# Gated linear attention into a gated SSM: all transfers on the sync queue, issued a few at a time, and the weights read a second time for their check

## Chip, cores and metric

One core of one Trainium2 chip. The metric is the device time of one execution in microseconds (us), median of several. An execution is called slow when it is over 1.5% above the fastest of the same kernel, and otherwise fast.

## The reference

For 4 batches of 8 heads, 768 steps and head dimension 48, a gated linear recurrence makes `y`. Its heads are joined to 384 channels and go through a gated state-space block of 512 inner channels:

```python
for t in range(S):                                        # S = 768
    state = alpha[:, :, t, :, None] * state + np.einsum('bhd,bhe->bhde', k[:, :, t], v[:, :, t])
    y[:, :, t] = np.einsum('bhd,bhde->bhe', q[:, :, t], state)
x = np.ascontiguousarray(y.transpose(0, 2, 1, 3)).reshape(B, S, H * D)
proj = x @ w_in;  val, gate = proj[..., :D_inner], proj[..., D_inner:]
h = a[0, 0] * h + val[:, t, :]                            # for each t; a = exp(A_log)
out = (silu(gate) * ys @ w_out).astype(np.float32)
```

The weights `w_in` and `w_out` arrive as float64. The kernel reads them as 32-bit words, builds float32 from them with integer operations, and checks that no weight lies outside the range for which this is right. If one does, a flag sends the kernel into a general, slow branch.

## The kernel before

The sequence is worked in 12 turns (4 batches of NG = 3 groups of 256 steps). Turn n handles the attention of group n, the projections (`pj`) of group n-1 and the output (`o`, `o_sb`, store) of group n-2. A hand-written list of letters gives the order of the parts of a turn: F and A are the front (scans, q, k, scores), B the back (states `z`, values `y`, features), P and H projection and scan, O the output, W the check of a part of the weights, L and M loads.

```python
early = ["FFFFLUFUFABBABB", "UUFPUUFHPUHFFPUHBBCPHABUAUBL", "FPUFHPUHFFPHBBCAPHBWAWOBWAWOM"]
usual = "FLPHPHFFOABBCPHABPHBAOM"

# the output: o_sb is in a pool of two buffers, the store goes out on ScalarE's queue
o_sb = pool.tile([C, DM], FP32, name="o_sb")
nc.scalar.activation(o_sb, o, AF.Copy)
nc.scalar.dma_start(out=out[b, ds(g * GC + c * C, C), :], in_=o_sb)

# from turn 4 on, alpha, q and k come by whole batches. staging (raw weights) and batches 1 and 3 share memory
t = big.tile([C, 3, NP * NW * W], FP32, tag=f"big{1 - b % 2}", name="batch")
...
nc.sync.dma_start(out=tv[...], in_=src[...])      # 48 for batch 1, 12 larger ones for batches 2 and 3
staging = big.tile([C, len(units), NK * C * 2], U32, tag="big0", name="staging")

def check_units(p):                               # in place, on the staged weights; four parts of 3 units
    h = staging[:, ds(WP * p, WP), :]...[:, :, 1].bitcast(FP32)
    nc.scalar.activation(h, h, AF.Square, scale=2.0 ** -16, accum_out=left_w[:, p, 0:1])
    nc.scalar.activation(h, h, AF.Relu, scale=-2.0 ** 60, bias=bias[:, 0:1], accum_out=left_w[:, p, 1:2])

def load_later(n):                                # the letter L
    ...
    if n in (NG, 2 * NG - 1):
        load_batch(2 if n == NG else 3)           # turns 3 and 5
def load_last(n):                                 # the letter M
    if n == 2:
        load_batch(1)
    if 2 <= n < N - 2:
        load(n + 2, "v", nc.scalar)               # v on ScalarE's queue
```

Of the kernel before, what the change touches and what calls it, by code (L numbers as in the profile page):

```python
# [9 lines left out]
FP32 = mybir.dt.float32  # L10
U8 = mybir.dt.uint8
U32 = mybir.dt.uint32
# [6 lines left out]
def kernel(  # L19
# [24 lines left out]
    nc = tc.nc  # L44
    B, H, S, D = q.shape
    DM = H * D
    DI = moe_A_log.shape[0]
    C = 128
    R = 64
    NR = C // R  # L50
    G = 2
    GC = G * C
    GR = G * NR
    NG = S // GC
    NP = H // 2
    DP = 64
    GP = G * NP
    NK = DM // C
    NI = DI // C
    N = B * NG  # L60
# [12 lines left out]
    w_out = const.tile([C, NI, DM], FP32, name="w_out")  # L73

    left = const.tile([C, N, 2], FP32, name="left")
    WP = 3
    left_w = const.tile([C, 3 * NI // WP, 2], FP32, name="left_w")
    flag = const.tile([1, 1], I32, name="flag")
    bias = const.tile([C, 3], FP32, name="bias")
# [3 lines left out]
    units = []  # L83
# [7 lines left out]
    def load_heads(dst, src, n, queue=nc.sync):  # L91

        b, g = divmod(n, NG)
        for c in range(G):
            rows = ds(g * GC + c * C, C)
            queue.dma_start(out=dst[:, c], in_=src[b, :, rows, :].rearrange("h p d -> p h d"))

    def load_pairs(dst, src, n, queue=nc.sync):

# [7 lines left out]
    def ssm(n, xT, prev_h, pool, ps_mm):  # L107

        b, g = divmod(n, NG)
        f = pool.tile([C, NI, GC], FP32, name="f")  # L110
        for cc in range(NI):
            pj = ps_mm.tile([C, 2, GC], FP32, tag="mm", name="pj")
            for i in range(2):
                for kk in range(NK):
                    nc.tensor.matmul(pj[:, i, :], w_in[:, kk, i, ds(cc * C, C)], xT[:, kk, :],  # L115
                                     start=(kk == 0), stop=(kk == NK - 1))
            yield
            hh = pool.tile([C, GC], FP32, tag=f"h{cc}", name="hh")
            nc.vector.tensor_tensor_scan(  # L119
                out=hh, data0=a_dec[:, cc:cc + 1].to_broadcast([C, GC]), data1=pj[:, 0, :],  # L120
                initial=prev_h[cc][:, GC - 1:GC] if g else 0.0, op0=ALU.mult, op1=ALU.add)
            prev_h[cc] = hh
            sg = pool.tile([C, GC], FP32, name="sg")
            nc.scalar.activation(sg, pj[:, 1, :], AF.Silu)  # L124
            nc.vector.tensor_mul(f[:, cc, :], sg, hh)  # L125
            yield
        for c in range(G):
            o = ps_mm.tile([C, DM], FP32, tag="mm", name="o")
            for cc in range(NI):
                nc.tensor.matmul(o, f[:, cc, ds(c * C, C)], w_out[:, cc, :],  # L130
                                 start=(cc == 0), stop=(cc == NI - 1))
            o_sb = pool.tile([C, DM], FP32, name="o_sb")
            nc.scalar.activation(o_sb, o, AF.Copy)  # L133
            nc.scalar.dma_start(out=out[b, ds(g * GC + c * C, C), :], in_=o_sb)
            yield

    def keys_back(K, Kn, ps_tp):
# [66 lines left out]
    def ranged(ctx):  # L204
        def pool(name, bufs, **kw):
            return ctx.enter_context(tc.tile_pool(name=name, bufs=bufs, **kw))

        own = pool("own", 1)
        p1 = pool("p1", 1)
        p2 = pool("p2", 2)  # L210
        p3 = pool("p3", 3)
# [18 lines left out]
        W = 32  # L230
        NW = S // W
        batches = {}

        def load_batch(b):
            t = big.tile([C, 3, NP * NW * W], FP32, tag=f"big{1 - b % 2}", name="batch")
            for m, (name, src) in enumerate((("a", alpha), ("q", q), ("k", k))):
                tv = t[:, m].rearrange("p (x e) -> p x e", e=W)
                batches[b, name] = t[:, m].rearrange("p (j x) -> p j x", j=NP)
                w0 = max(0, BY_VECTOR - NG * b) * GC // W
                for i in range(2):  # L240
                    nc.gpsimd.memset(tv[ds(DP * i + W, W), :, D - W:W], 1.0 if name == "a" else 0.0)  # L241
                for j, nj in [(0, NP)] if w0 == 0 else [(j, 1) for j in range(NP)]:
                    for i in range(2):
                        for half in range(2):
                            ch = min(W, D - W * half)
                            nc.sync.dma_start(  # L246
                                out=tv[ds(DP * i + W * half, W), j * NW + w0:(j + nj) * NW, 0:ch],
                                in_=src[b, ds(NP * i + j, nj), w0 * W:S, ds(W * half, ch)]
                                .rearrange("j (w p) d -> p (j w) d", p=W))

        vs, st, xs = {}, {}, {}

        def load(n, names="aqkv", queue=nc.sync):
            for name in names:
                if name == "v":
                    vs[n] = p3.tile([C, G, H, D], FP32, name="v_sb")
                    load_heads(vs[n], v, n, queue)
                elif n < BY_VECTOR:
                    load_pairs(pads[n % NBUF][name], dict(a=alpha, q=q, k=k)[name], n, queue)

        staging = big.tile([C, len(units), NK * C * 2], U32, tag="big0", name="staging")
# [19 lines left out]
                                           op0=ALU.bitwise_and, op1=ALU.bitwise_or)  # L281
            nc.gpsimd.tensor_add(units[u][0].bitcast(I32), units[u][0].bitcast(I32), lo.bitcast(I32))

        def check_units(p):


            h = staging[:, ds(WP * p, WP), :].rearrange("p u (x two) -> p (u x) two", two=2)[:, :, 1].bitcast(FP32)
            nc.scalar.activation(h, h, AF.Square, scale=2.0 ** -16, accum_out=left_w[:, p, 0:1])
            nc.scalar.activation(h, h, AF.Relu, scale=-2.0 ** 60, bias=bias[:, 0:1], accum_out=left_w[:, p, 1:2])

# [86 lines left out]
        def check_products(n):  # L377
            V = Vs[n % 2]
            junk = p1.tile([C, NP, GC], U8, name="junk")
            nc.scalar.activation(junk, V[:, :, 0:GC], AF.Relu, scale=-1.0 / LOW, bias=bias[:, 0:1],  # L380
                                 accum_out=left[:, n, 0:1])
            nc.scalar.activation(junk, V[:, :, 0:GC], AF.Relu, scale=1.0 / HIGH, bias=bias[:, 2:3],
                                 accum_out=left[:, n, 1:2])
# [58 lines left out]
        for u in range(4, 8):  # L442
            fetch_unit(u)
        nc.scalar.activation(a_dec, a_log, AF.Exp)
        to_convert, to_check = iter(range(len(units))), iter(range(len(units) // WP))

        def any_outside():

            worst = own.tile([C, 1], FP32, name="worst")
            bad = own.tile([C, 3 * NI // WP * 2 + 1], FP32, name="bad")  # L450
            nc.vector.tensor_reduce(out=bad[:, 0:1], in_=left.rearrange("p n w -> p (n w)"),
# [12 lines left out]



        early = ["FFFFLUFUFABBABB", "UUFPUUFHPUHFFPUHBBCPHABUAUBL", "FPUFHPUHFFPHBBCAPHBWAWOBWAWOM"]
        usual = "FLPHPHFFOABBCPHABPHBAOM"
        ending = ["PHPHOPHPHO", "OO"]
        fronts = {n: front(n) for n in range(N)}  # L470
        backs = {n: back(n) for n in range(N)}
        ssms = {}

        def load_later(n):
            if n < 2:
                load(n + 2)
            if n == 0:
                for u in range(8, len(units)):
                    fetch_unit(u)
            if n in (NG, 2 * NG - 1):  # L480
                load_batch(2 if n == NG else 3)

        def load_last(n):
            if n == 2:
                load_batch(1)
            if 2 <= n < N - 2:
                load(n + 2, "v", nc.scalar)

        with tc.manual_schedule():
            for n in range(N + 2):  # L490
                if n == N:
                    any_outside()
                for word in early[n] if n < len(early) else usual if n < N else ending[n - N]:
                    if word == "F":
                        step(fronts[n])
                    elif word == "A":
                        step(fronts.get(n + 1))
                    elif word == "B":
                        step(backs[n])
                    elif word in "PH":  # L500
                        if n - 1 not in ssms:
                            ssms[n - 1] = ssm(n - 1, xs.pop(n - 1), prev_h, p2, ps_mm)
                        step(ssms[n - 1])
                    elif word == "O":
                        step(ssms[n - 2])
                    elif word == "C":
                        if n == 1:
                            check_products(0)
                        check_products(n)
                    elif word == "U":  # L510
                        convert_unit(next(to_convert))
                    elif word == "W":
                        check_units(next(to_check))
                    elif word == "L":
                        load_later(n)
                    elif word == "M":
                        load_last(n)
            outside = nc.values_load(flag[0:1, 0:1], min_val=0, max_val=1)
        return outside

# [189 lines left out]
```

## Time and profile before

| | before |
|---|---|
| time, median of 3 runs | 336.53 us (334.48 to 337.38) |
| span of the profiled execution | 334.8 us |
| mean clock of TensorE (1 is full) | 0.942 |
| TensorE busy | 291.8 us, 87% |
| VectorE busy / ScalarE busy | 67% / 38% |
| read from HBM | 23.60 MB |

TensorE (PE) is the engine to watch. The lines that show where it is not full, and what each turn costs, stand in the prediction.

### The profile page before, as it was taken

The numbers are of one execution on the slowest core, as the hardware profiler recorded it, in microseconds if no ns is written. First come the engines' busy times: TensorE is split into PE (matmuls) and PEld (weight loads), VectorE is DVE, ScalarE is ACT, GpSimd is POOL, SyncE is SP. The second block draws the span as 40 slices with busy tenths as digits, with TensorE's granted clock in tenths as the row PEclk, the third lists the DMA queues.
The fourth block names the chain that finished last, engine by engine and source line by source line (L and its number), as shares of the span: only waits on it lengthen the run. The fifth ranks groups of instructions, "written<-read, shape, count | busy, mean of one in ns | idle before, by whom it ended". The sixth has DMA issues, their size and how long they took to land.

```text
span 334.8 us, 9254 instructions
## 1 busy us (share of the span) xinstructions
PE 291.8 (87%) x4041; PEld 231.6 (69%) x4041; DVE 223.5 (67%) x387; ACT 126.0 (38%) x259; POOL 45.0 (13%) x58
## 2 busy tenths in 40 slices
PE   1577995899499792599999999999999999999993
PEld 1355883787377671477787778877887778777771
DVE  1886786769123960679878888898788988833220
ACT  1133668237932410243252442513524325244111
POOL 4020420320069300000910000000000000000000
PEclk9995898699789898599999999999999999999999
DMA  9999994000056547976885996940030120000011
GB/s 129 224 223 239 204 222 86 0 3 4 23 104 99 72 74 99 125 101 94 116 117 108 132 120 99 153 79 31 2 72 25 28 46 25 25 26 2 27 45 59
DMA packets 157570, 29.01 MB, mean 87 GB/s; under 512 B 150864, under 2 KB 157008, under 8 KB 157520
## 3 DMA queue, kind: packets, MB, share of 16 engines
q1 hardware_dynamic: 134784, 20.06, 41.2%
q10 hardware_dynamic: 22736, 8.26, 10.1%
q8 instruction: 34, 0.56, 0.7%
q14 instruction: 16, 0.13, 0.1%
HBM read 23.60 MB, written 4.72 MB: 85 GB/s over the span
## 4 chain that ended last, share of the span: by engine, by line
PE 75%; DVE 6%; DMA 6%; ACT 5%; SPq 3%; issue 3%; ACTq 1%; DVEq 0%
PE pj L115 34%; PE o L130 18%; PE sc L368 4%; PE tp L326 4%; PE tpk L142 4%; PE y L187 4%; PE z L154 3%; PE y L169 3%; DMA v_sb<-in_v_dram 3%; PE tpx L196 3%; SPq L246 2%; DVE P L344 2%; DVE V L339 2%; DMA pads<-in_alpha_dram 1%; DMA batch<-in_q_dram 1%
## 5 line engine op out<-in xcount | busy, mean ns | idle before, releaser
L115 PE MATMUL pj<-xT,w_in 128*128 128x256 f32 x576 | 135.6, 389 | 0.0
L115 PEld LDWEIGHTS pj<-xT,w_in 128*128 128x128 f32 x576 | 109.7, 194 | 17.6 <-issue 0.2
L130 PE MATMUL o<-w_out,f 128*128 128x384 f32 x192 | 67.9, 499 | 0.0
L124 ACT ACTIVATE sg<-pj 128x256 f32<-128x256 f32 x48 | 18.4, 384 | 119.1 <-DVE hh L119 98.6
L130 PEld LDWEIGHTS o<-w_out,f 128*128 128x128 f32 x192 | 36.2, 197 | 20.9 <-issue 2.1
L119 DVE TENSOR_TENSOR_SCAN hh<-a_dec,hh,pj 128x256 f32<-128x256 f32 x32 | 23.7, 740 | 21.1 <-PE pj L115 21.1
L125 DVE TENSOR_TENSOR f<-sg,hh 128x256 f32<-128x256 f32 x48 | 20.4, 425 | 24.9 <-ACT sg L124 24.9
L326 PE MATMUL tp<-ident,pads 128*128 128x128 f32 x96 | 19.6, 358 | 16.0 <-DMA pads<-in_alpha_dram 6.9
L241 POOL MEMSET batch<- 32x1536 f32 x18 | 24.7, 1371 | 64.7 <-DMA out_dram<-o_sb 41.7
L326 PEld LDWEIGHTS tp<-ident,pads 128*128 128x128 f32 x96 | 15.0, 183 | 19.4 <-issue 8.0
L368 PE MATMUL sc<-Q,K 64*64 64x64 f32 x768 | 15.9, 237 | 10.7 <-DVE K L359 10.6
L133 ACT ACTIVATE o_sb<-o 128x384 f32<-128x384 f32 x24 | 11.8, 490 | 33.5 <-PE o L130 33.5
L368 PEld LDWEIGHTS sc<-Q,K 64*64 64x64 f32 x768 | 14.0, 148 | 14.9 <-issue 14.3
L344 DVE TENSOR_TENSOR_SCAN P<-aT,iV,bias 128x256 f32<-128x256 f32 x32 | 23.6, 780 | 0.6
L339 DVE TENSOR_TENSOR_SCAN V<-aT,bias 128x256 f32<-128x256 f32 x32 | 20.3, 677 | 0.3
L393 POOL TENSOR_TENSOR S_n<-S_end,V 128x192 f32<-128x192 f32 x7 | 4.2, 598 | 118.5 <-DVE V L339 118.5
L330 DVE STREAM_TRANSPOSE K<-batch 128x1024 f32<-128x1024 f32 x8 | 9.9, 1239 | 12.7 <-DMA batch<-in_k_dram 12.7
L196 PE MATMUL tpx<-ident,x_sb 128*128 128x128 f32 x72 | 11.9, 300 | 6.0 <-DVE P L344 4.3
L187 PEld LDWEIGHTS y<-S_n,Q 64*64 64x64 f32 x704 | 13.1, 140 | 5.7 <-issue 4.9
L169 PE MATMUL y<-v_sb,A 64*64 64x48 f32 x768 | 14.2, 220 | 3.2 <-issue 3.2
L371 DVE COPY_PREDICATED A<-mask,sc 128x512 f32<-128x512 uint8 x24 | 16.1, 723 | 0.7 <-PE sc L368 0.7
L154 PEld LDWEIGHTS z<-v_sb,Kn 64*64 64x64 f32 x768 | 12.3, 134 | 6.1 <-issue 5.4
(64 smaller groups left out, 314.2 us busy)
## 6 DMA issues: line engine op xcount, KB each, us to landing
out_dram<-o_sb ACTq DMA_DIRECT2D x24, 192.0 KB, 2.0
staging<-in_moe_w_in_dram SPq DMA_DIRECT2D x8, 384.0 KB, 5.0
v_sb<-in_v_dram ACTq DMA_DIRECT2D x16, 192.0 KB, 3.4
pads<-in_alpha_dram SPq DMA_DIRECT2D x16, 96.0 KB, 5.0
pads<-in_k_dram SPq DMA_DIRECT2D x16, 96.0 KB, 3.7
v_sb<-in_v_dram SPq DMA_DIRECT2D x8, 192.0 KB, 4.4
staging<-in_moe_w_out_dram SPq DMA_DIRECT2D x4, 384.0 KB, 5.5
batch<-in_alpha_dram SPq DMA_DIRECT2D x4, 384.0 KB, 6.6
```

What stands on the lines that cost most here:

```text
L115: nc.tensor.matmul(pj[:, i, :], w_in[:, kk, i, ds(cc * C, C)], xT[:, kk, :], start=(kk == 0), stop=(kk == NK - 1))
L119: nc.vector.tensor_tensor_scan(out=hh, data0=a_dec[:, cc:cc + 1].to_broadcast([C, GC]), data1=pj[:, 0, :], initial=prev_h[cc][:, GC - 1:GC ...
L130: nc.tensor.matmul(o, f[:, cc, ds(c * C, C)], w_out[:, cc, :], start=(cc == 0), stop=(cc == NI - 1))
L154: nc.tensor.matmul(zv[chs, r, g, j, :], Kn[rows, g, j, chs], v_sb[rows, g, NP * i + j, :], start=True, stop=True, skip_group_check=True)
L169: nc.tensor.matmul(yv[at, i, c, j, :], A[rows, i, c * NP + j, :], v_sb[rows, c, NP * i + j, :], start=(c == 0 and j == 0), stop=False, ski ...
L187: nc.tensor.matmul(yv[at, i, c, j, :], Q[rows, j, ds(R * x, R)], S_n[rows, x, j, :], start=False, stop=(c == G - 1 and j == NP - 1), skip_ ...
L196: nc.tensor.transpose(tp[:, kk, :], x_sb[:, c, ds(kk * C, C)], ident)
L241: nc.gpsimd.memset(tv[ds(DP * i + W, W), :, D - W:W], 1.0 if name == "a" else 0.0)
L326: nc.tensor.transpose(tp[:, u, ds(c * C, C)], pad[name][:, c, j], ident)
L339: nc.vector.tensor_tensor_scan(out=V[:, 2 * jj + u, GC - 1::-1], data0=tp[:, u, ::-1], data1=bias[:, 1:2].to_broadcast([C, GC]), initial=1 ...
L344: nc.vector.tensor_tensor_scan(out=P[:, 2 * jj + u, :], data0=tp[:, u, :], data1=bias[:, 1:2].to_broadcast([C, GC]), initial=iV0[:, 2 * jj ...
L368: nc.tensor.matmul(scv[ds(R * r, R), i, c * NP + j, :], K[rows, j, steps], Q[rows, j, steps], start=True, stop=True, skip_group_check=True)
```

## The change

The intent is to free the memory of the staged weights earlier, so that batch 1 can be loaded earlier, and to keep transfers from waiting for one another across two queues. (1) The check leaves turn 2. From turn 4 on, two units (768 KB) at a time are read again into a small tile `part` and checked a turn later. (2) Every transfer goes to the sync queue. (3) Loads are put in a list, and each letter L takes up to eight of them (turns up to 3) or two (later). (4) The lists of letters get more L's, and in turn 2 the q of the next turn is transposed sooner; a check of products (C) moves from turn 1 to turn 0.

```diff
-    WP = 3
+    WP = 2
@@ ssm
-            nc.scalar.dma_start(out=out[b, ds(g * GC + c * C, C), :], in_=o_sb)
+            nc.sync.dma_start(out=out[b, ds(g * GC + c * C, C), :], in_=o_sb)
@@
+        waiting = []
+        def issue(most):
+            for _ in range(min(most, len(waiting))):
+                dst, src = waiting.pop(0)
+                nc.sync.dma_start(out=dst, in_=src)
@@ load_batch
-                            nc.sync.dma_start(out=tv[...], in_=src[...])
+                            waiting.append((tv[...], src[...]))
@@ check_units becomes
+        def fetch_part(p):
+            parts[p] = p1.tile([C, WP, NK * C * 2], U32, name="part")
+            for w in range(WP):
+                dst, src = units[WP * p + w]
+                waiting.append((parts[p][:, w].rearrange("p (a n) -> p a n", a=dst.shape[1]), src.bitcast(U32)))
+        def check_part(p):
+            h = parts.pop(p).rearrange(...)          # then the same two activations
@@
-        early = ["FFFFLUFUFABBABB", "UUFPUUFHPUHFFPUHBBCPHABUAUBL", "FPUFHPUHFFPHBBCAPHBWAWOBWAWOM"]
-        usual = "FLPHPHFFOABBCPHABPHBAOM"
+        early = ["FFFFGUFUFCABBABB", "UUFPUUFGHPUHFFPUHBBCPHABUAUB", "PFHPFUHUFFAPHBMBCPHALBAOLBOL"]
+        usual = "FLPHPLHFFOLABMBCLPHABLPHBAWLO"
@@ the letter M (make_ready)
+            if n in (2, NG, 2 * NG - 1):
+                load_batch({2: 1, NG: 2, 2 * NG - 1: 3}[n])
+            if n + 2 < N:
+                vs[n + 2] = p3.tile([C, G, H, D], FP32, name="v_sb")
+                load_heads(vs[n + 2], v, n + 2, waiting)
+            if 0 <= n - NG - 1 < len(units) // WP:
+                fetch_part(n - NG - 1)
@@ the letters
+                    elif word == "W" and n - NG - 2 in parts:
+                        check_part(n - NG - 2)
+                    elif word == "L":
+                        issue(8 if n <= NG else 2)
```

More of the change, by code (lines that the diff above doesn't have):

```diff
@@ L95, in load_heads @@
             rows = ds(g * GC + c * C, C)
-            queue.dma_start(out=dst[:, c], in_=src[b, :, rows, :].rearrange("h p d -> p h d"))
+            pair = dst[:, c], src[b, :, rows, :].rearrange("h p d -> p h d")
+            if isinstance(queue, list):
+                queue.append(pair)
+            else:
+                queue.dma_start(out=pair[0], in_=pair[1])
     def load_pairs(dst, src, n, queue=nc.sync):
@@ L245, in load_batch @@
                             ch = min(W, D - W * half)
-                            nc.sync.dma_start(
-                                out=tv[ds(DP * i + W * half, W), j * NW + w0:(j + nj) * NW, 0:ch],
-                                in_=src[b, ds(NP * i + j, nj), w0 * W:S, ds(W * half, ch)]
-                                .rearrange("j (w p) d -> p (j w) d", p=W))
+                            waiting.append((tv[ds(DP * i + W * half, W), j * NW + w0:(j + nj) * NW, 0:ch],
+                                            src[b, ds(NP * i + j, nj), w0 * W:S, ds(W * half, ch)]
+                                            .rearrange("j (w p) d -> p (j w) d", p=W)))
         vs, st, xs = {}, {}, {}
@@ L282, in convert_unit @@
             nc.gpsimd.tensor_add(units[u][0].bitcast(I32), units[u][0].bitcast(I32), lo.bitcast(I32))
-        def check_units(p):
-            h = staging[:, ds(WP * p, WP), :].rearrange("p u (x two) -> p (u x) two", two=2)[:, :, 1].bitcast(FP32)
+        parts = {}
+        def fetch_part(p):
[4 more added lines that the diff above has]
+        def check_part(p):
+            h = parts.pop(p).rearrange("p u (x two) -> p (u x) two", two=2)[:, :, 1].bitcast(FP32)
             nc.scalar.activation(h, h, AF.Square, scale=2.0 ** -16, accum_out=left_w[:, p, 0:1])
@@ L444, in ranged @@
         nc.scalar.activation(a_dec, a_log, AF.Exp)
-        to_convert, to_check = iter(range(len(units))), iter(range(len(units) // WP))
+        to_convert = iter(range(len(units)))
         def any_outside():
@@ L472, in ranged, with load_group @@
         ssms = {}
-        def load_later(n):
-            if n < 2:
-                load(n + 2)
+        def load_group(n):
+            load(n + 2)
             if n == 0:
@@ L479, in load_later, with make_ready @@
                     fetch_unit(u)
-            if n in (NG, 2 * NG - 1):
-                load_batch(2 if n == NG else 3)
-        def load_last(n):
-            if n == 2:
-                load_batch(1)
-            if 2 <= n < N - 2:
-                load(n + 2, "v", nc.scalar)
+        def make_ready(n):
+            if n in (2, NG, 2 * NG - 1):
[5 more added lines that the diff above has]
+                fetch_part(n - NG - 1)
         with tc.manual_schedule():
@@ L506, in ranged @@
                     elif word == "C":
-                        if n == 1:
-                            check_products(0)
                         check_products(n)
@@ L511, in ranged @@
                         convert_unit(next(to_convert))
-                    elif word == "W":
-                        check_units(next(to_check))
+                    elif word == "W" and n - NG - 2 in parts:
+                        check_part(n - NG - 2)
+                    elif word == "G":
+                        load_group(n)
                     elif word == "L":
-                        load_later(n)
+                        issue(8 if n <= NG else 2)
                     elif word == "M":
-                        load_last(n)
+                        make_ready(n)
             outside = nc.values_load(flag[0:1, 0:1], min_val=0, max_val=1)
```

## The prediction

> **What bounds the kernel now.** I read the page first (row PE of the tenths), then the busy time by stretch, one per turn, then the chain of waits from 95 to 138 us, then the waits of the sync queue (SPq).
>
> ```profile
> PE   1577995899499792599999999999999999999993
> DMA  9999994000056547976885996940030120000011
> 60.60:95.10 34.50, 29.95 (x367) 23.75 (x368) 19.16 (x36) 20.34 (x37) 4.29 (x5) 0.86 0.02 7
> 95.10:121.90 26.80, 24.84 (x327) 19.63 (x326) 16.88 (x29) 8.26 (x18) 16.47 (x13) 0.94 0.63 94
> 121.90:156.40 34.50, 23.93 (x336) 19.24 (x335) 18.16 (x31) 8.48 (x18) 0.00 (x0) 0.85 0.83 107
> 156.40:178.20 21.80, 21.80 (x336) 17.38 (x335) 18.37 (x31) 8.31 (x18) 9.04 (x7) 1.00 0.72 101
> ```
>
> The last four lines are turns 2, 3, 4 and 5 (stretch, length, then busy us of PE, PEld, DVE, ACT, POOL, clock, DMA share, GB/s). From turn 5 on a turn is 21.8 us of unbroken TensorE at full clock, so nothing can be won there. Turns 2 to 4 are 12.7, 5.0 and 12.7 us longer. While they run too long, DMA has spare time (share 0.02, 0.63, 0.83): data come late because they are asked for late.
>
> ```profile
> SPq L246 <- ACT staging L289: 42.3, 1, 42.3
> SPq L246 <- DMA out_dram<-o_sb: 29.1, 7, 7.6
> SPq L246 <- DMA v_sb<-in_v_dram: 19.8, 7, 7.9
> ...
> 122.62 0.36 ACTq L134
> ...
> 123.52 3.97 DMA v_sb<-in_v_dram
> ...
> 132.64 2.64 DMA batch<-in_k_dram
> ...
> 135.69 1.26 DVE K L330
> ...
> 137.81 2.07 PE sc L368 x64
> ```
>
> The sync queue stands 42.3 us before the first transfer of batch 1, because its memory is held by the staged weights until their check (L288/L289, on ScalarE in turn 2) is done. Afterwards it waits in total 48.9 us for stores and v loads of ScalarE's queue: the eight completion semaphores go round over both queues, so a load of L246 cannot be issued before an earlier ScalarE transfer has landed, and that one stands behind ScalarE's work. So k comes at 135.3 and TensorE idles 10.57 us in turn 4.
>
> **What the Trainium skill says.** "DMA: Bandwidth & Descriptors", section "Issuing engines are not separate DMA queues": transfers of all issuers run on the same 16 engines, and a second issuer saves only sequencer time. The trace agrees: one issue takes 0.49 us. The same page, section "Queues, rings and completion order", says that each engine goes round between the queues that have work, and takes descriptors of one queue in ring order. So a store on ScalarE's queue passes a heap of loads on the sync queue, and one on the sync queue does not. The first half agrees with the trace: stores land after a median of 2.0 us while batch loads take 6.6 to 7.5; the second half is not shown yet. "TensorE: Matmul & The Clock Gate", section "Part 1: The HAM clock gate", puts a lower clock after idle windows: after the 10.57 us of idle, sc takes 2.07 instead of 1.09 us.
>
> **The change part by part.**
>
> *Checks out of turn 2.* Four pairs of L288/L289 (1.26 + 1.33 us and two accumulator reads of 0.19) go: 8 instructions, 10.3 us of ScalarE between 82.0 and 94.4. They delayed o_sb and xT, and TensorE idled 4.28 us at 88.80 and was slow after it. But the new order of turn 2 puts the transposes of q (A) right behind those of alpha. Written out with the durations of before, VectorE is busy without break from about 68 us; its scan P ends 4.7 us after the fourth pj, while TensorE has only y and four transposes (2.0 us) to do: a new idle time of some 2.6 us, with a slow o behind it. One check of two moves from turn 1 to turn 0, where ScalarE idles 5.9 us: two of 1.27 us less ahead of sg at 53.93, of which 1.55 count, as sg also waits for hh (ends 52.3). So turn 3 starts at about 92.3 instead of 95.1: 2.8 won.
>
> *Turns 3 and 4.* Staging is free at the last conversion (about 71 us), so alpha of batch 1 is issued there and between the two stores of turn 2. After the second store (turn 3's start S3 + 1.0) come 24 issues at 0.53, store 3, and eight of k: 0.9 + 12.8 + 0.4 + 4.3 = S3 + 18.4, landing 2.6 later at S3 + 21. K is wanted at S3 + 23.6: the waits for alpha, q and k go. Turn 3 then takes 22.3 (steady plus its transposes of k) and turn 4 takes 21.8, so turn 5 starts at 92.3 + 44.1 = 136.4 instead of 156.4: 20.0 us won in all.
>
> *What is given back, turn 5.* In turn 3 eight are still issued at each place, so all 12 large transfers of batch 2 (3072 descriptors each) and two of v stand on the sync queue ahead of the second store of turn 3 (order of instructions: rows 115 to 128, the store at 129). They begin at S3 + 20.3. Between 134 and 147 us the sync queue moved 15942 descriptors in 13 us, 2.5 us for one such transfer; its best stretches give 2.2. Twelve take 27 to 30 us, v 1.7, the store 0.6 + 1.3: it lands at S3 + 51 to 54. Its buffer o_sb (two of them) is needed by the second o of turn 4, which ends at S3 + 44.1; TensorE can do one pj more (until 46.7) before it needs the PSUM that o_sb has not emptied. So turn 5 stalls 5 to 8 us, and some 2 us of slow clock follow: 6.5 to 10.
>
> *Given back, turn 6.* From turn 4 on two are issued at a place. Batch 3 (12 transfers) begins after the first store of turn 5, 9.5 us before turn 6 (S6), and stands ahead of v and of the second part of the weights. 30 us of batch, two stores (1.2), v 1.7, part 3.2 and receipt 1.3: the part lands at S6 + 24.7 to 27.9. Its check is wanted at S6 + 19.7 and takes 2.1 (estimate from L288/L289 by 768 of 1152 elements); it is ahead of o_sb on ScalarE, and TensorE can wait only until S6 + 24.4. Stall 3 to 6 us, with the clock 4.5 to 8.
>
> *Rest.* 4.7 MB more are read, in long rows, some 3 us of DMA in each of six turns. The checks add 12.5 us to ScalarE (busy 38%). Other turns stay at 21.8.
>
> Sum: -20.0 + 6.5..10 + 4.5..8 = -9 to -2 us, that is 327.5 to 334.5 from 336.5.
>
> **The rivals.** (a) *No stall after turn 4.* If stores aren't held up by loads ahead of them, or the transfers run at 1.9 us each (128-byte rows at 216 GB/s in the best stretches), store 4 lands at about S3 + 46.7 and just misses harm; the gain of 20 us stays and the time is 316 to 318. For it: issuing a few at each place looks like a schedule tuned against just this. Against it: the mean of 2.5 and the ring order. (b) *The queue becomes the bound.* If back-pressure makes a transfer 2.8 us or more, each of the stalls grows by 3 to 4 us, and turn 2 may win nothing: 337 to 342. For it: issues of L246 lasted up to 3.6 us, and a store now waits in line behind them. Against it: no second queue mixes in. (c) *The second read itself costs.* The engines are at 0.7 to 1.0 in turns 5 to 8; but it has a turn of slack except in turn 6, so it costs only there. (d) *VectorE as the bound of turn 2.* If its chain is shorter than written out, turn 2 wins up to 5 us more.
>
> **Range and chances.** The sum's middle is 331; (a), which I give three in ten, pulls it down, (b), one in ten, up: 329.5. The limit of 2% faster is 329.8, close to the middle, and so faster is only a little over even. Eight in ten: 317 (a) to 338 (a mild b).
>
> **What would show it.** Right: alpha, q and k of batch 1 no longer in the chain; turns 3 and 4 of about 22 us; ScalarE's o_sb waiting for a store at the start of turn 5, with TensorE idle 5 to 8 us in pj; the check of a part waiting for its load at the end of turn 6, TensorE idle 3 to 6 us; all later turns 21.8. Wrong: the wait for k still there (then issues take longer than 0.53); turns 5 and 6 of 21.8 (stores are not held up: near 317); idle time in turns 7 to 10 (the weights cost); turn 2 shorter than 30 us (d).

## The result and the profile after

The changed kernel takes 351.23 us (349.83 to 352.92, 4 runs) against 335.5 (332.16 to 337.38, 4 runs) for the kernel before on the same chip. The ratio is 1.0506, with a 95% interval of 1.0402 to 1.061: slower, and the prediction was wrong. Throughout, a ratio is the mean time of one kernel's fast runs over that of the other's of the same rounds, so it is not quite the ratio of the medians quoted. The profiled spans are 349.0 after and 334.8 before.

Two rows of the page of the kernel after, in 40 slices of 8.7 us:

```profile
PE   1567995987999999009999935999999999999992
DMA  9999982030566999994599996203332130000111
```

The row of TensorE is full from the eleventh slice on, where before it had a 4, a 2 and a 5, but it has a new hole of two slices ("00") and one of a slice and a half ("35"). The table of stretches has one line per turn, for turns 2 to 7 (stretch, length, busy us of PE, PEld, DVE, ACT and POOL, clock, DMA share, GB/s):

```profile
59.05:91.90 32.85, 28.31 (x367) 22.62 (x368) 19.28 (x37) 9.84 (x21) 11.76 (x10) 0.93 0.14 22
91.90:114.50 22.60, 22.60 (x327) 18.20 (x326) 16.06 (x28) 8.28 (x18) 8.75 (x7) 1.00 0.70 99
114.50:136.30 21.80, 21.80 (x336) 17.36 (x334) 18.75 (x32) 8.38 (x18) 0.52 (x1) 1.00 1.18 116
136.30:178.90 42.60, 24.85 (x336) 19.07 (x335) 18.41 (x31) 8.87 (x19) 8.23 (x6) 0.76 0.93 117
178.90:201.00 22.10, 22.05 (x319) 17.51 (x318) 18.89 (x32) 9.60 (x22) 0.52 (x1) 1.00 1.22 119
201.00:234.65 33.65, 23.84 (x336) 18.55 (x334) 18.44 (x32) 10.74 (x23) 0.52 (x1) 0.85 0.56 103
```

Turns 3 and 4 are now free of stalls, and turn 5 starts at 136.30, where before it started at 156.40: 20.1 us won. Then turn 5 lasts 42.60 instead of 21.80 (TensorE's busy time rose from 21.80 to 24.85 at a lower clock, and the other 17.75 are idle), and turn 7 lasts 33.65 (2.04 of slow clock and 9.81 idle). Two lines of TensorE's order of time, then two of ScalarE's, show these holes. The bracket is the idle time ahead of the group and what ended it:

```profile
156.80 5.49 PE L119 MATMUL pj<-xT,w_in 128*128 128x256 f32 x12 [17.75 <-ACT o_sb L137]
213.56 4.65 PE L119 MATMUL pj<-xT,w_in 128*128 128x256 f32 x12 [9.81 <-ACT o_sb L137]
```

```profile
156.26 0.49 ACT L137 ACTIVATE o_sb<-o 128x384 f32<-128x384 f32 x1 [20.51 <-DMA out_dram<-o_sb]
211.06 0.90 ACT L308 ACTIVATE part<-part 128x768 f32<-128x768 f32 x1 [10.80 <-DMA part<-in_moe_w_in_dram]
```

TensorE waits both times for `o_sb`, which empties the PSUM buffer that `pj` needs. But `o_sb` itself waits in turn 5 for a store to free its buffer, and in turn 7 stands on ScalarE behind a check whose part has not landed. The order of time of the sync queue (start, length of the group, count) tells why the store and the part are late:

```profile
94.07 0.43 SPq L138 DMA_DIRECT2D out_dram<-o_sb  x1
94.55 9.74 SPq L244 DMA_DIRECT2D batch<-in_q_dram  x16
...
115.36 10.64 SPq L244 DMA_DIRECT2D batch<-in_alpha_dram  x4
126.04 11.14 SPq L244 DMA_DIRECT2D batch<-in_q_dram  x4
137.22 11.38 SPq L244 DMA_DIRECT2D batch<-in_k_dram  x4
148.65 3.80 SPq L244 DMA_DIRECT2D v_sb<-in_v_dram  x2
152.55 1.23 SPq L138 DMA_DIRECT2D out_dram<-o_sb  x2
```

For 33.3 us the queue does nothing but issue the twelve large transfers of batch 2, 2.77 us each, where a small one takes about half a microsecond. The store that frees `o_sb` can only be *issued* at 152.55. Over the whole kernel a store lands a median of 2.1 us after its issue (2.0 before), so a store is not slow once it is issued; what it lacks is its turn.

The waits of the sync queue (total, times, longest) answer to those of before:

```profile
SPq L138 <- ACT o_sb L137: 93.3, 12, 12.6
SPq L244 <- ACT o_sb L137: 22.3, 2, 11.3
SPq L244 <- POOL w_out L293: 21.6, 1, 21.6
```

The wait of 42.3 us for the staged weights is down to 21.6 (for the last conversion), and the 48.9 us in which loads stood waiting for stores and v of the other queue are gone, as intended. What stands in their place are waits for `o_sb`: of stores for their data, and of two loads late in the kernel (22.3 us, all after 225 us). They cost nothing by themselves while nothing behind them is wanted.

### The profile page after: what moved, and what is told of

It is laid out like the page before. It is cut to its first block, busy times and chain, and to the rows that moved or that the text cites. A ratio compares the mean times of both kernels' runs of the same rounds, so it can differ in the third digit from the quotient of the medians.

```text
span 349.0 us, 9297 instructions
## 1 busy us (share of the span) xinstructions
PE 290.4 (83%) x4041; PEld 229.7 (66%) x4041; DVE 223.1 (64%) x387; ACT 126.6 (36%) x267; POOL 44.5 (13%) x58
## 5 line engine op out<-in xcount | busy, mean ns | idle before, releaser
L119 PE MATMUL pj<-xT,w_in 128*128 128x256 f32 x576 | 140.3, 398 | 28.1 <-ACT o_sb L137 27.6
L119 PEld LDWEIGHTS pj<-xT,w_in 128*128 128x128 f32 x576 | 112.0, 199 | 47.9 <-ACT o_sb L137 28.4
L134 PE MATMUL o<-w_out,f 128*128 128x384 f32 x192 | 65.6, 486 | 0.0
L134 PEld LDWEIGHTS o<-w_out,f 128*128 128x128 f32 x192 | 34.9, 190 | 19.7
L123 DVE TENSOR_TENSOR_SCAN hh<-a_dec,hh,pj 128x256 f32<-128x256 f32 x32 | 23.7, 739 | 27.7 <-PE pj L119 27.7
L346 PE MATMUL tp<-ident,pads 128*128 128x128 f32 x96 | 17.9, 333 | 15.4 <-DMA pads<-in_alpha_dram 7.0
L253 POOL MEMSET batch<- 32x1536 f32 x18 | 24.7, 1373 | 17.2 <-PE tp L346 10.1
L346 PEld LDWEIGHTS tp<-ident,pads 128*128 128x128 f32 x96 | 13.7, 169 | 18.7 <-issue 10.8
L364 DVE TENSOR_TENSOR_SCAN P<-aT,iV,bias 128x256 f32<-128x256 f32 x32 | 23.7, 780 | 0.6
L359 DVE TENSOR_TENSOR_SCAN V<-aT,bias 128x256 f32<-128x256 f32 x32 | 20.3, 676 | 0.3
L388 PE MATMUL sc<-Q,K 64*64 64x64 f32 x768 | 15.3, 230 | 0.6 <-DVE K L379 0.3
L359 DVE TENSOR_TENSOR_SCAN V<-tp,bias 128x256 f32<-128x256 f32 x16 | 10.1, 673 | 8.9 <-PE tp L346 8.9
L123 DVE TENSOR_TENSOR_SCAN hh<-a_dec,pj 128x256 f32<-128x256 f32 x16 | 10.8, 677 | 7.6 <-PE pj L119 7.6
```

Source lines behind the costliest of these rows:

```text
L119: nc.tensor.matmul(pj[:, i, :], w_in[:, kk, i, ds(cc * C, C)], xT[:, kk, :], start=(kk == 0), stop=(kk == NK - 1))
L123: nc.vector.tensor_tensor_scan(out=hh, data0=a_dec[:, cc:cc + 1].to_broadcast([C, GC]), data1=pj[:, 0, :], initial=prev_h[cc][:, GC - 1:GC ...
L134: nc.tensor.matmul(o, f[:, cc, ds(c * C, C)], w_out[:, cc, :], start=(cc == 0), stop=(cc == NI - 1))
L253: nc.gpsimd.memset(tv[ds(DP * i + W, W), :, D - W:W], 1.0 if name == "a" else 0.0)
L346: nc.tensor.transpose(tp[:, u, ds(c * C, C)], pad[name][:, c, j], ident)
L359: nc.vector.tensor_tensor_scan(out=V[:, 2 * jj + u, GC - 1::-1], data0=tp[:, u, ::-1], data1=bias[:, 1:2].to_broadcast([C, GC]), initial=1 ...
```

## The experiments

My theory T: the gain is real and comes from freeing the staged weights; the loss comes from *order in one queue*, because things wanted soon (a store that frees a buffer, v, a part) stand behind a heap of transfers wanted later. Rivals: R1, the engines are full and any order stalls somewhere; R2, the second read's bytes or checks cost; R3, it is the stores alone, and putting them back on ScalarE's queue mends all.

**1. Six buffers for o_sb.**

```diff
+        p_out = pool("p_out", 6)
-            o_sb = pool.tile([C, DM], FP32, name="o_sb")
+            o_sb = (o_pool or pool).tile([C, DM], FP32, name="o_sb")      # o_pool = p_out
```

> The changed kernel with six o_sb buffers instead of two; queue, order and pacing as changed. Theory A (turn 5 stalls because ScalarE cannot empty the second o of turn 4: its o_sb buffer still belongs to a store that stands on the sync queue behind the 12 loads of batch 2): ScalarE no longer waits for out_dram at the start of turn 5, the 17.75 us of idle in pj is gone. But the v of turn 5 was issued at 148.65 to 152.5 behind the same loads and landed at about 155, and z of turn 5 would then want it at about 147: a new wait of z for v_sb of about 8 us, with 2 us of slow clock. Turn 7 keeps its 10 to 12 us (part late). Time 351 - 20.8 + 10 = about 340. Rival R1 (the DMA engines are simply full, the buffer is a symptom): the time stays within 2 us of 351, with the idle time moved to other waits. Rival R2 (the second read of the weights costs the time): no change in turn 5, 351.

Measured 345.64 us (344.44 to 346.51), before 337.14; ratio 1.0252 (1.0187 to 1.0318). TensorE's order of time:

```profile
156.06 1.96 PE L158 MATMUL z<-v_sb,Kn 64*64 64x48 f32 x64 [9.49 <-DMA v_sb<-in_v_dram]
208.47 5.49 PE L119 MATMUL pj<-xT,w_in 128*128 128x256 f32 x12 [14.52 <-ACT o_sb L137]
```

The wait for the store is gone from turn 5. In its place TensorE waits 9.49 us for v, the next thing behind the heap, and turn 7's stall grows from 9.81 to 14.52: TensorE stops there 9.8 us earlier than in the changed kernel (at 193.95 instead of 203.75), but the part's check can start only 5.1 us earlier (205.98 instead of 211.06). The time is thus 5.6 us above the 340 that I expected. More buffers move the wait on; they do not take it away.

**2. Stores back on ScalarE's queue.**

```diff
-            nc.sync.dma_start(out=out[b, ds(g * GC + c * C, C), :], in_=o_sb)
+            nc.scalar.dma_start(out=out[b, ds(g * GC + c * C, C), :], in_=o_sb)
```

> The changed kernel with one line undone: the output stores are issued on ScalarE's queue again. Theory A: stores pass the heap of loads, so the o_sb wait of turn 5 is gone; the sync queue is no longer held up by waiting for stores, so batch 2 and v of turn 5 come some 5 us earlier and z waits for v_sb at most 1 to 2 us; batch 3 begins at the start of turn 5, so the part of turn 6 lands close to when its check is wanted and turn 7 stalls 0 to 3 us. The completion semaphores shared by both queues bring some ScalarE waits of a few us that hide. Time 317 to 323, faster than the kernel before by 4 to 5 per cent. R1 (engines full): still 345 or more, as the bytes and descriptors are the same. R2 (second read): turn 7 keeps its 12 us, about 335.

Measured 346.40 us (345.19 to 347.17); ratio 1.0275 (1.021 to 1.0339). My expectation missed by over 20 us. TensorE's order of time, then one line of the sync queue's waits:

```profile
124.07 1.44 PE L388 MATMUL sc<-Q,K 64*64 64x64 f32 x64 [2.90 <-DVE K L379]
161.39 2.16 PE L158 MATMUL z<-v_sb,Kn 64*64 64x48 f32 x64 [10.41 <-DMA v_sb<-in_v_dram]
210.05 5.38 PE L119 MATMUL pj<-xT,w_in 128*128 128x256 f32 x12 [9.03 <-ACT o_sb L137]
```

```profile
SPq L244 <- DMA out_dram<-o_sb: 19.0, 6, 6.0
```

The stores now get by, but v and the part still stand behind the heap (10.41 and 9.03 us of idle TensorE), and the old coupling is back: the sync queue waits 19.0 us for stores of the other queue, so k is late again. R3 falls.

**3. Parts 2 to 6 one turn later.**

```diff
-            if 0 <= n - NG - 1 < len(units) // WP:
-                fetch_part(n - NG - 1)
+            if n in PART_AT:                 # {4: 0, 6: 1, 7: 2, 8: 3, 9: 4, 10: 5}
+                fetch_part(PART_AT[n])
-                    elif word == "W" and n - NG - 2 in parts:
-                        check_part(n - NG - 2)
+                    elif word == "W" and PART_AT.get(n - 1) in parts:
+                        check_part(PART_AT[n - 1])
```

> The changed kernel with the second to sixth part of the weights read and checked one turn later (turns 7 to 11), so that none is behind batch 3 and wanted in the same turn; everything else as changed. Theory A: turn 7 loses its 11.9 us over a steady turn, turn 5 keeps its 20.8; time about 339. R2 (the bytes of the second read load the engines and that is what costs): the 12 us only move to other turns, time within 2 us of 351. R1: as R2.

Measured 341.17 us (339.15 to 341.83); ratio 1.0137 (1.0076 to 1.0198). TensorE's order of time still has the hole of turn 5, and none of turn 7:

```profile
156.83 4.84 PE L119 MATMUL pj<-xT,w_in 128*128 128x256 f32 x12 [16.68 <-ACT o_sb L137]
```

The same parts are fetched and checked, and the 10 us are back. So the loss of turn 7 is the place of one part behind batch 3, not the bytes. This speaks against R2.

**4. Before without the check (a mistake).** I took the check out of the kernel before and filled its result with 1.0.

```diff
-        early = [..., "FPUFHPUHFFPHBBCAPHBWAWOBWAWOM"]
+        early = [..., "FPUFHPUHFFPHBBCAPHBAOBAOM"]
+        nc.gpsimd.memset(left_w, 1.0)
```

> The kernel before without the check of the weights in turn 2 (the flag's inputs are filled with 1.0, so the output is still right for these inputs, but the guard is gone); all queues, orders and pacing as before. It asks which part of the 20.1 us that the change wins by the start of turn 5 comes from freeing the staging memory and ScalarE alone. Theory A': nearly all of it; batch 1 starts at about 71 instead of 95 us, and the 12.7 us of turn 4, the 5 us of turn 3 and most of the 4 to 6 us of idle in turn 2 go, with v and stores still on ScalarE's queue and no new stall: 312 to 318. Rival: the moving of v and stores to the sync queue is what lets k come in time (the shared completion semaphores hold L246 back): the wait for k in turn 4 stays at 5 us or more and the time is 322 to 328.

Measured 1062.31 us. The guard takes a value of 0.5 or more for "outside", so the general branch ran as well. It says nothing; run 7 repeats it with 0.0.

**5. V first, six buffers, parts later.** On the edits of runs 1 and 3, v of the next turns is listed ahead of the batch.

```diff
-            if n in (2, NG, 2 * NG - 1):
-                load_batch({2: 1, NG: 2, 2 * NG - 1: 3}[n])
             if n + 2 < N:
                 vs[n + 2] = p3.tile([C, G, H, D], FP32, name="v_sb")
                 load_heads(vs[n + 2], v, n + 2, waiting)
+            if n in (2, NG, 2 * NG - 1):
+                load_batch({2: 1, NG: 2, 2 * NG - 1: 3}[n])
```

> The changed kernel with three repairs: v of a turn is put on the waiting list ahead of the batch of the same turn, six o_sb buffers, and the second to sixth part of the weights one turn later. Queue, pacing (eight at a place to turn 3, then two) and bytes as changed. Theory B (one queue in ring order makes what is wanted soon - v, stores, a part - wait behind 33 us of batch that is wanted a turn later; nothing else is lost): all of the 20.8 us of turn 5 and 11.9 of turn 7 go, turns 4 to 10 are 21.8, and 351 - 33 = 318. Rival R1 (the DMA engines have too much to do in turns 3 to 6 and any order leaves something late): a new wait of 5 us or more turns up in turns 4 to 7, time 325 or more.

Measured 325.21 us (320.1 to 327.67), before 336.92; ratio 0.9682 (0.961 to 0.9754). In the profiled execution (320.1, the fastest) the largest idle time that TensorE has for a transfer or `o_sb` after turn 4 is 1.11 us. The other three runs took 324.4 to 327.7, and two of them, 326.04 and 327.67, are slow against the 320.1. The ratio still has them: it is the mean of these three over that of the kernel before. The two fast runs alone, 320.10 and 324.38, lie 4.2% below the kernel before, so it is faster either way. I have no profile of one of the longer runs, so that spread stays unexplained, and with it whether they kept a wait of 5 us.

**6. V first, two a place, parts later, two buffers of o_sb.** As run 5, but o_sb keeps its two buffers. Instead, only the first three places of turn 3 issue eight, and from then on two are issued at a place, so that stores come between. It is three edits at once; which of them mends what is read from runs 1 to 3.

```diff
-                        issue(8 if n <= NG else 2)
+                        issue(8 if n < NG or (n == NG and places < 3) else 2)
+                        places += 1
```

> The changed kernel with v ahead of the batch, the parts one turn later as before, two o_sb buffers as changed, and in turn 3 eight transfers at the first three places only, two at the last three. Theory B: four to six of the large transfers (2.8 us each) stand ahead of a store, which then lands within 15 us of being ready, while its buffer is wanted 22 us later; no stall, 318 as f1. If the buffers of o_sb and not the place in the queue were the matter, this run would keep a wait of o_sb for out_dram of 5 us or more (325 or more) while f1 would not.

Measured 322.68 us (321.1 to 323.51); ratio 0.9573 (0.9508 to 0.9639). The sync queue of this run, in order of time, over the stretch of batch 2:

```profile
114.33 3.77 SPq L244 DMA_DIRECT2D batch<-in_alpha_dram  x2
118.20 2.78 SPq L138 DMA_DIRECT2D out_dram<-o_sb  x1
121.03 3.47 SPq L244 DMA_DIRECT2D batch<-in_alpha_dram  x2
124.54 5.45 SPq L244 DMA_DIRECT2D batch<-in_q_dram  x2
130.09 2.79 SPq L138 DMA_DIRECT2D out_dram<-o_sb  x1
132.92 2.96 SPq L244 DMA_DIRECT2D batch<-in_q_dram  x2
135.92 12.09 SPq L244 DMA_DIRECT2D batch<-in_k_dram  x4
```

The transfers are as slow as before (the last four take 3.0 us each), and even a store's issue now lasts 2.8 us, but it comes after two transfers and not after twelve. One line of TensorE's order of time is left of the two holes, where I had expected none (and 318 us):

```profile
161.08 4.54 PE L119 MATMUL pj<-xT,w_in 128*128 128x256 f32 x12 [2.05 <-ACT o_sb L137]
```

With the same bytes, the same queue, the same second read and the same two buffers, 28.6 us are gone against the changed kernel (351.23, another chip). In the profiled executions 4.2 of the 27.9 us lie ahead of the scores of turn 1 (41.89 and 37.69), which no edit explains (see run 11); behind them 23.7 are gone (307.1 and 283.4). R1 falls, and R2 can hold at most for a few microseconds.

**7. Before without the check, this time right.** As run 4, with the result filled with 0.0. It has no guard and is a measurement, not a candidate.

> As e4, mended: e4 filled the flag's inputs with 1.0, which the guard takes as out of range, so the general branch ran too (1062 us); now 0.0. The kernel before without the check of the weights in turn 2. Theory A': batch 1 starts at about 71 instead of 95 us, and turns 3 and 4 lose their waits with v and stores still on ScalarE's queue: 312 to 320, and the wait of K in turn 4 is gone. Rival (shared completion semaphores of two queues hold L246 back, as e2 showed on a small scale: 19 us of waits for out_dram and K late by 2.9 us): K still waits 5 us or more, 322 to 330.

Measured 317.65 us (315.02 to 319.54); ratio 0.9452 (0.9386 to 0.9518). TensorE's order of time has one idle time of over 1 us from 70 us on:

```profile
116.29 1.53 PE L368 MATMUL sc<-Q,K 64*64 64x64 f32 x64 [3.63 <-DVE K L359]
```

Two queues, the old order, and yet most of the gain. The wait for k, 10.57 us before, is 3.63, which is neither gone (my theory) nor 5 us or more (the rival). The sync queue still waits 35.2 us for stores and 19.5 for v of ScalarE's queue. Of the 21.6 us between the profiled spans, 3.8 lie ahead of the scores of turn 1, where the check has no part. Counted from there to the start of turn 5, this run wins 17.9 us on the kernel before and the changed kernel 20.3. So most of the gain is the freed staging and ScalarE (not told apart here). The difference is the sum of two things that no run separates. From the scores of turn 3 to those of turn 4, where k is waited for, this run takes 25.46 us and the changed kernel 21.76; from the scores of turn 2 to those of turn 3 it takes 25.40 and the changed kernel 29.20, since the new order of turn 2 has idle times of its own (1.55 and 2.52 us, for Kn and for scan P). The runs that beat both kernels from the changed side, 5 and 6, still carry this order; no run took it out.

**8. Before with only the stores on the sync queue.**

```diff
-            nc.scalar.dma_start(out=out[b, ds(g * GC + c * C, C), :], in_=o_sb)
+            nc.sync.dma_start(out=out[b, ds(g * GC + c * C, C), :], in_=o_sb)
```

> The kernel before with one line of the change: the output stores on the sync queue, nothing else. Theory B: the stores of turn 3 and 4 stand behind 48 small and 12 large transfers of batches 1 and 2, which are issued in one go; they land after about 160 us, so o_sb of turn 4 waits for a buffer some 10 to 20 us, and the store heap behind batch 3 does the same once more around turn 6 to 7; the semaphore waits for ScalarE's stores go, which brings K some us earlier. Time 345 to 370. Rival (queue order doesn't matter): 330 to 338.

Measured 356.58 us (355.37 to 357.44); ratio 1.0598 (1.0532 to 1.0663). A line of the waits, and one of TensorE's order of time:

```profile
ACT o_sb L133 <- DMA out_dram<-o_sb: 28.9, 2, 22.1
```

```profile
161.63 1.96 PE L187 MATMUL y<-S_n,Q 64*64 64x48 f32 x64 [15.11 <-ACT fence L174]
```

One line of source costs 20 us in a kernel with nothing else changed. ScalarE stands 22.1 us at o_sb for a store behind the heap of batch 2, and TensorE then waits for the small ScalarE operation that comes after it (`fence`). This is the loss by itself, shown without the second read.

**9. The second read, with the old queues.** The kernel before, with the check taken out of turn 2 and the parts of run 3 put in. Stores and v stay on ScalarE's queue.

```diff
-        early = [..., "FPUFHPUHFFPHBBCAPHBWAWOBWAWOM"]
-        usual = "FLPHPHFFOABBCPHABPHBAOM"
+        early = [..., "FPUFHPUHFFPHBBCAPHBAOBAOM"]
+        usual = "FLPHPHFFOABBCPHABPHBAWOM"
+                nc.sync.dma_start(out=parts[p][:, w]..., in_=src.bitcast(U32))    # in M of turns 4, 6 to 10
```

> The kernel before with the check taken out of turn 2 and the second read with its check put into later turns (parts fetched in turns 4, 6 to 10, checked a turn later), but with stores and v left on ScalarE's queue and every batch issued at one place as before. Result right, guard whole. If the gain is all in the freed staging and ScalarE, and the second read rides along beside other work: 316 to 321 us, like the run without any check (317.65), with its K wait of about 3.6 us and no wait of a part's check over 2 us. If the second read's 4.7 MB cost something by themselves: 325 us or more, with idle time in pj in turns 5, 7 to 11.

Measured 323.0 us (321.31 to 323.8), before 334.98; ratio 0.9665 (0.9579 to 0.975). This is some 2 us above my range, with no idle time over 1.44 us in pj. Two lines of TensorE's order of time carry what the check costs:

```profile
163.38 2.86 PE L115 MATMUL pj<-xT,w_in 128*128 128x256 f32 x12 [1.44 <-ACT o_sb L133]
...
292.96 0.27 PE L466 MATMUL wt<-ident,worst 128*1 128x128 f32 x1 [1.24 <-DVE worst L464]
```

Set against run 7 by the starts of the scores of each turn, the profiled span is 6.4 us longer (319.6 to 313.2). Of this, 2.2 lie ahead of turn 1, 0.6 in the turn of k, 1.7 in the turn of the first check (23.5 instead of 21.8), and 2.0 after the last scores, where the last check stands before the flag. So the second read costs about 4 us in these two executions; the rest is in the start-up, where it has no part.

**10. The same, v of turn 4 earlier.** The letter M of turn 2 moves from the end to the middle.

```diff
-        early = [..., "FPUFHPUHFFPHBBCAPHBAOBAOM"]
+        early = [..., "FPUFHPUHFFPHBMBCAPHBAOBAO"]
```

> The run beside it, with the one difference that the word that loads batch 1 and v of turn 4 stands in the middle of turn 2, not at its end; batch 1 is then issued at the same time as before it (when staging is free), but v of turn 4 leaves ScalarE's queue some 10 us earlier. If the sync queue's remaining waits, which hold k of batch 1 back, are waits for v of ScalarE's queue through the shared completion semaphores, the K wait of 3.6 us falls to under 1.5 us and the time to 313 to 318. If they are waits for the stores, nothing moves: within 1 us of the run beside it.

Measured 325.04 us (322.39 to 325.94); ratio 0.9726 (0.9641 to 0.9812). It is 2.0 us above run 9, where I had expected 313 to 318 or a time within 1 us. V of turn 4 leaves at 74.15 instead of 87.98, and yet the wait for k is 3.85 us (3.60 in run 9), so it is not this v that holds k back. In the stretch of batch 1 the sync queue waits 14.1 us for stores and 4.7 for v (15.3 and 3.2 in run 9). That the stores hold k back in the two-queue version is thus likely and not shown: I did not take their waits away by an experiment.

**11. Four parts instead of six.**

```diff
-    WP = 2
+    WP = 3
-        PART_AT = {4: 0, 6: 1, 7: 2, 8: 3, 9: 4, 10: 5}
+        PART_AT = {6: 0, 7: 1, 8: 2, 9: 3}
```

> The same as the run with the parts in later turns and the old queues (323.0), but with four parts of three units, as the check of before has them, fetched in turns 6 to 9 and checked in turns 7 to 10. That run lost 1.7 us in turn 5 to a part's check and 2.0 us at the end, where the last check stood before the flag. If those are what the second read costs, the time falls by 3 to 4 us: 318 to 321. If a part of 1152 elements (2.6 us of ScalarE) holds o_sb back by itself, idle time in pj of over 1 us shows in turns 7 to 10 and the time stays at 322 or more.

Measured 321.76 us (321.36 to 324.18), before 335.22; ratio 0.9626 (0.955 to 0.9702). The waits of turn 5 and ahead of the flag are gone as expected. But the time fell by only 1.2 us, and one reason stands at the front of TensorE's order of time:

```profile
27.25 0.67 PE L169 MATMUL y<-v_sb,A 64*64 64x48 f32 x12 [3.86 <-issue]
```

This idle time in turn 0 ("issue": TensorE waited for nothing that the profile shows) is 3.86 us here and 3.3 in run 9, 3.04 before and 3.59 after the change; run 6 has 0.65 of it and run 7 none. The edits of runs 6, 9 and 11 don't touch turn 0 (run 7 puts a memset into the start-up). So comparisons of profiled spans can carry up to 4 us of start-up, and I can't say whether that belongs to the kernel or to the execution. From the scores of turn 1 to the end the spans are 278.2 here, 279.5 in run 9 and 275.3 in run 7, so even there only 1.3 of the 3 to 4 us are won. The parts of three units cost something too: between the scores of turns 7 and 8 this run takes 22.79 us (0.75 idle in pj), between those of turns 9, 10 and 11 22.06 and 22.11, where run 7 takes 21.78, and after the last scores 43.62 to 42.57.

| run | time us | ratio to before | what it tells |
|---|---|---|---|
| changed kernel | 351.23 | 1.0506 | |
| 1 six o_sb | 345.64 | 1.0252 | wait moves to v |
| 2 stores on ScalarE's queue | 346.40 | 1.0275 | v, part and k wait |
| 3 parts later | 341.17 | 1.0137 | turn 7 mended, 10 us |
| 5 v first, six o_sb, parts later | 325.21 | 0.9682 | both holes mended |
| 6 v first, paced, parts later | 322.68 | 0.9573 | the same with two o_sb |
| 7 before, no check | 317.65 | 0.9452 | most of the gain by itself |
| 8 before, stores on sync | 356.58 | 1.0598 | the loss by itself |
| 9 before, second read | 323.0 | 0.9665 | guard kept, old queues |
| 10 as 9, v earlier | 325.04 | 0.9726 | v of turn 4 doesn't hold k |
| 11 as 9, four parts | 321.76 | 0.9626 | guard kept, old queues |

Runs 6, 9 and 11 beat both kernels with the guard whole; their intervals overlap, and I rank none above the others.

## Why the prediction was wrong

**The gain was right.** Turn 3 was to start at 92.3 and starts at 91.90; turn 5 was to start at 136.4 and starts at 136.30. 20.0 us were to be won by then, and 20.1 were. The new idle time in turn 2, some 2.6 us, came too (2.52, for scan P). Run 7 shows that most of the gain comes from the freed staging and ScalarE.

**The step that failed is "What is given back, turn 5".** Mechanism and place were right: o_sb waits for a store behind batch 2, and TensorE idles in pj. The size was off, 6.5 to 10 predicted and 20.8 measured (17.75 idle, 3.05 of slow clock). Counted from the start of turn 3 (S3), the store landed at +64.3 instead of +51 to +54, and three terms of that sum were too small:

| term | predicted | measured | off by |
|---|---|---|---|
| batch 2 begins | S3 + 20.3 | S3 + 23.5 | 3.2 |
| twelve transfers | 27 to 30 | 33.3 | 4.8 from the middle |
| v and the store | 3.6 | 7.6 | 4.0 |

The first was late because the second store of turn 2 was issued at S3 + 2.2, not S3 + 1.0, and because the 24 issues after it took 14.7 us, not 12.8. The second was 2.77 us for a transfer. I had taken 2.5 from a stretch of the kernel before and given weight to its best, 2.2; nothing in the new order promised the best. The third was the most avoidable. I counted v and the store as if the queue were empty behind the heap, but they are issued into the same backlog: v's two issues took 3.8 us, and the last store landed 3.7 us after v's issues ended. The stall takes an excess of 12 us in full, because TensorE's slack ends at a fixed time (S3 + 46.7). A small error in each of three terms of a long serial sum more than doubled what was left after subtracting the slack.

**"Given back, turn 6" failed the same way.** 4.5 to 8 predicted, 11.85 measured (9.81 idle and 2.04 of slow clock). The check could start at S6 + 32.2 instead of S6 + 24.7 to 27.9. The twelve transfers were right this time (28.7 us). Of the rest, two stores took 4.35 us instead of 1.2, v 3.7 instead of 1.7, and the part 6.2 instead of 4.5, all issued into the backlog; the batch began 1.25 us earlier than I had it, which took a little back. The estimate of the check itself, 2.1 us, was right.

**One term was left out:** from the end of the last `o` on TensorE to the end of the kernel it is 6.3 us after and 5.0 before. The store's queue needn't be the cause, as runs 9 to 11, with stores on ScalarE's queue, have 5.7 to 6.2. The sum of the spans is then -20.1 + 20.8 (turn 5) + 0.3 (turn 6) + 11.85 (turn 7) + 1.3 = +14.2, which is 349.0 - 334.8.

**The rivals.** (b), the queue becomes the bound, was the right one, and I gave it one in ten: transfers took 2.77 us, its figure. Even so I made it 337 to 342, because it carried only the transfer term and not the issues into the backlog. (a) was wrong although the schedule looked tuned against this: from turn 4 on it was paced, but turn 3 was not. Run 6 shows that pacing turn 3 too, with v first and the parts later, removes the holes but for 2.05 us. (c), the second read costs, was right as it was put: it cost in the one turn without slack (10 us, run 3) by its place, and with slack some 4 us or less (runs 9 and 11). (d) is not seen: turn 2 lasts 32.85 us. The centre of 329.5 was also too high for its own weights: 317 at three in ten, 339.5 at one and 331 at six make 327.7, so a prediction true to its own weights would have missed by more.

**What stays open.** Why a large transfer takes 2.77 us in this stretch and 2.4 in that of batch 3. It is not the work of issuing: the first of batch 3, which finds little ahead of it, is issued in 0.37 us (at 168.15), and the next takes 3.83. The kinds with 64-byte rows (192 KB) land as late after their issue (8.6 to 9.3 us) as those with 128-byte rows (384 KB, 8.3 to 8.9), so it does not go with bytes (both kinds have 3072 rows); but the DMA share falls for about 1 us between transfers while the sequencer is busy without break, and no run told why. Also open are the spread of run 5, the start-up of 0 to 4 us, and what the new order of turn 2 costs (run 7).

## What to carry to other kernels

Before moving a transfer to a busy queue, list what will stand ahead of it and when its result is wanted: the sum of what stands ahead, less the slack of who waits, is the stall, so let it be small items first and large ones a few at a time. When a change has a gain and a loss of about one size, size the loss's terms under load, not from quiet stretches, and put the errors of all its terms on the difference, not on the sum. And separate a bundle: here one of its parts held most of the gain (run 7), and another, alone, costs 6% (run 8).

## What the Trainium skill lacked or had wrong

- The Trainium skill's page "DMA: Bandwidth & Descriptors", section "Issuing engines are not separate DMA queues", says that a second issuer only saves sequencer time, "which is usually small relative to the DMA itself". An issue with little ahead of it is small here too (0.37 us at 168.15). But behind a backlog that time is the matter: issues of twelve transfers held the sequencer 33.3 us (2.77 each, up to 3.85), and moving only the stores from ScalarE to it made the kernel 6% slower (run 8).
- The same page, section "Queues, rings and completion order", describes the order in the rings. The trace agrees that later transfers of the queue come later, but the greater part of a store's delay is ahead of the ring: it was issued only at 152.55 us, and stores landed a median of 2.1 us after their issue. I found no page that says how much a hardware queue takes in before an issue blocks; here about three large transfers were under way at once (8.4 us from issue to landing, one issued every 2.77).
- I found no page that says that transfers of two queues that share completion semaphores hold each other up. In the traces the transfers of both queues share eight (100 and 102 to 108). Before, the sync queue waited 48.9 us in total for stores and v of ScalarE's queue, and in run 2 it waited 19.0 us for stores.
